# Two MLP layers behind windowed attention: the first four tiles' softmax divided after the product with the values

## The chip, the cores and the metric

The kernel runs on one core of one Trainium2 chip. The metric is the device time of one execution in microseconds (us), the median of several runs. The engines are TensorE (PE: matrix products; PEld is its loading of weights), VectorE (DVE), ScalarE (ACT), GpSimd (POOL) and SyncE (SP, which issues the DMA transfers). Each works through its own list of instructions in order and waits on semaphores for the others.

## The reference

```python
def _attn_ref(q, k, v):              # 4 batches, 8 heads, 576 positions, 64 per head
    ...
    mask = (rel >= 0) & (rel < 64)   # a window of 64 positions
    scores = np.where(mask, scale * (q @ k^T), -1e9)
    attn = np.exp(scores - max(scores))
    attn = attn / (sum(attn) + 1e-09)
    return attn @ v

def reference(...):
    x = attention output as (2304 tokens, 512)
    x = (s * relu(x @ moe_w_in)**2 + b) @ moe_w_out       # 512 -> 2048 -> 512
    h = x @ moe2_w_in
    return np.maximum(0.01 * h, h) @ moe2_w_out           # 512 -> 2048 -> 512
```

The weights arrive as 64-bit floats and are turned into 32-bit ones on the chip. Products are made as three passes of rounded parts (high by high, high by low, low by high), so that the result keeps 32-bit accuracy.

## The kernel before

**Tiles.** Attention is computed in 18 tiles of 128 tokens. Tile i goes through these operations, whose names the planner uses: `lq`, `lk`, `lv` (loads), `sc` (scores on PE, in two groups g of four heads), `mm` (DVE: mask and minimum, one instruction per head), `exp` (ACT, one per head, with the row's sum taken along by `accum_out`), `inv` (DVE: add 1e-9, reciprocal), `norm` (multiply by the reciprocal), `tp` (PE: transpose the weights of attention), `tt` (ACT: copy them to SBUF as `pt`), `pv` (PE: the product with the values, which leaves x transposed in PSUM as `xps`), `xh` (ACT: rounded high part of x) and `xl` (DVE: the rest). For the first four tiles (`early`, the first block of 512 tokens) `norm` is one DVE instruction per group (`normalise_four`); for later tiles it is eight ACT instructions.

**Steps of the first layer.** The first layer works in steps: one block of tokens by one chunk of 128 hidden units, 16 chunks. Step s makes `h` (lines 525 to 535: eight products with the high weights, four with the low), `e` 0 to 3 (ACT and DVE in turn: relu, square and scale, high part, low part) and `y` (lines 555 to 568: twelve products into four accumulators). Block 0 runs chunks 0 to 7, then block 1 all 16, then block 0 the rest. Each chunk's weights are loaded once (`lw`), converted (`cv` 0 on ACT, `cv` 1 to 4 on DVE, lines 451 to 470) and split into `wh` (ACT, line 487) and `wl` (DVE, line 493). Step s < 8 therefore needs chunk s freshly converted; the steps of block 1 that follow, 8 to 15, use the same eight chunks again.

**What sets the order.** `Order.emit` is a planner: every operation has an engine, an estimated duration, a rank (`key`, lower goes first), what it comes after, and the buffers that it takes. The planner plays the program through with these estimates and emits, on each engine, the ready operation of lowest rank. `self.fill(...)` tells the PE's gaps to `fill`, which puts products of zeros (line 1115) into a gap, until step 7's first activation is emitted. The PSUM pool "a" has four buffers: one is held by the `warm` tile of the zeros until step 0's second accumulator is done, two are used by `sc` of tiles 1 and 3, and `xps` of the first four tiles takes one each.

**Chunk 0** is loaded and converted in two halves, so its instructions are 512 wide and not 1024. `raw` has two buffers, so a chunk's load waits for the conversion of the chunk two before.

Of the kernel before, what the change touches and what calls it, by code (L numbers as in the profile page):

```python
# [15 lines left out]
P = 128  # L16
H, D = 8, 64
# [109 lines left out]
def kernel(  # L127
# [35 lines left out]
    sbt = const.tile([P, 2], F32, name="sbt")  # L163
    ydr = dramp.tile([P, KD, T], F32, name="ydr")
# [40 lines left out]
    EARLY = BLOCKS1[0] // P  # L205
    q_t, k_t, v_t, s_t, sc_t, sum_t, nmax_t, x_t, pt_t, tp_t = ({} for _ in range(10))
# [103 lines left out]

# [23 lines left out]
    def add_attention(i, b, t0, key):  # L334
# [17 lines left out]
        add(name("lv"), "sp", 1600, key - 4, lambda: load_v(i),  # L352
# [7 lines left out]
        for g in range(2):  # L360
            add(name("sc", g), "pe", 700, key - 6, lambda g=g: scores(i, g, sc),
# [5 lines left out]
            for j in range(4):  # L367
                add(name("mm", g, j), "dve", 172, key - 4.87, lambda g=g, j=j: mask_max(i, g, j),
                    [name("sc", g)] + ([name("mm", 0, 0)] if g + j else after_v) + [("masks",)],
                    first if g + j == 0 else (), [("sc", i, j % 2), ss, ("sm", i)])  # L370
                add(name("exp", g, j), "act", 480, key - 3.07, lambda g=g, j=j: exponent(i, g, j),
                    [name("mm", g, j)], use=[ss, ("sm", i)])

            if i < 2:
# [6 lines left out]
            if early:  # L381
# [8 lines left out]
            add(name("tp", g), "pe", 560, key - 2.96, lambda g=g: transpose_pe(i, g, tp),  # L390
                norm + [("masks",)], [(tp, "tp", i, g)], [ss])
            add(name("tt", g), "act", 478, key - 5.69, lambda g=g: take_transposed(i, g),
# [3 lines left out]
            add(name("pv", g), "pe", 620, key - 1, lambda g=g: values(i, g, xt),  # L396
                last + [name("lv")] + ([name("pv", 0)] if g else []),
                () if g else [(xt, "xt", i)], [("xt", i), ("v", i), pt])
        if i >= IN_W:
# [5 lines left out]
        add(name("xh"), "act", 478, key - 0.1, lambda: split_x_hi(i, b, t0),  # L405
# [3 lines left out]
        add(name("xl"), "dve", 602, key - 0.1, lambda: split_x_lo(i, b, t0),  # L409
# [193 lines left out]
    def add_step(s):  # L603
# [4 lines left out]
        for j in range(halves):  # L608
# [4 lines left out]
            add(("h", s, 0, j), "pe", 1820 * fj, s - 0.6, lambda c0=c0, c1=c1: emit_h(s, 0, c0, c1),  # L613
                [w_done["wh", l, c, 0]] + xs + ([("h", s, 1, j - 1)] if j else []),
                () if j else [("h", "h", s)], [("h", s), hi, *x])
            add(("h", s, 1, j), "pe", 910 * fj, s - 0.6, lambda c0=c0, c1=c1: emit_h(s, 1, c0, c1),
                [w_done["wl", l, c, 0], ("h", s, 0, j)], (), [("h", s), lo, *x])
        add(("e", s, 0), "act", 60 + 420 * f, s - 0.9, lambda: activate(s, 0),
            [("h", s, 1, halves - 1)], [("g", k, s) for k in ("r", "gh", "gl")], [("h", s)])
        add(("e", s, 1), "dve", 60 + 600 * f, s - 0.9, lambda: activate(s, 1),  # L620
            [("e", s, 0), ("sbt",)], use=[("r", s)])
        add(("e", s, 2), "act", 100 + 500 * f, s - 0.9, lambda: activate(s, 2),
            [("e", s, 1)], use=[("r", s), ("gh", s)])
        add(("e", s, 3), "dve", 60 + 600 * f, s - 0.9, lambda: activate(s, 3),
# [4 lines left out]
        if c0 < c < c1 - 1:  # L629
            both = [("y", s, 0), ("y", s, 1)]  # L630
            add(both[0], "pe", 2 * count * ns, s + 0.5,
# [469 lines left out]
    def masks():  # L1101
        make_masks()
        make_identity(nc, ident)

# [35 lines left out]
    for c in range(KF):  # L1140
        key = first_step[0, c, "w"] - 2.5
        if c == 0:
            add_weights(0, c, 0, 1, key - 4, -10.21)
            add_weights(0, c, 1, 2, key - 3.75, -11.71)
        else:
            add_weights(0, c, 0, 2, key + (-0.16 if c < 4 else 0))
# [3 lines left out]
    for b, n in enumerate(BLOCKS1):  # L1150
        for j in range(n // P):
            if b == 0:
                key = 1.0 * j - 6
            elif b == 1:
                key = 2 * j + 1.75
            else:
                key = first_step[0, 2] - 10 + 2 * (i - IN_W)
# [84 lines left out]
```

## Time and profile before

| | |
|---|---|
| median of 3 runs | 840.34 us (839.98 to 841.68) |
| the profiled execution's own time | 838.37 us |
| its span | 836.6 us |
| busy share of the span | PE 99%, PEld 88%, DVE 72%, ACT 53%, POOL 0% |
| first product of the first layer starts | 32.17 us |
| DMA | 194.65 MB, mean 233 GB/s |

The span runs from the first instruction to the last; what lies around it is 1.77 us. Busy shares are means over stages with different limits: DVE's 72% holds stretches where it has no gap. In a row of the time line, the first number is the start, the second the duration until the last result is out, and in brackets stands the idle time before it and what ended that. Two instructions that follow each other on one engine overlap at their ends, so the cost of one is read from start to start. In a view by windows the columns are: stretch in us, its length, then busy us (and instructions) of PE, PEld, DVE, ACT and POOL, the granted clock of TensorE as a share of its higher level of 2.4 GHz, the DMA share and GB/s. In a view by groups they are: line, engine, operation, names and shapes, count | busy us, mean ns of one | idle us before it and what ended it. A 32-bit product with small operands shows as two records, each with its own load of weights.

### The profile page before, as it was taken

To read this page: it belongs to the slowest core of one execution; us is meant where nothing else is said; L and a number is where in the kernel's file an instruction comes from. 1 tells how busy PE (TensorE), PEld (TensorE's weight loads), DVE (VectorE), ACT (ScalarE), POOL (GpSimd) and SP (SyncE) were. 2 spreads that over 40 slices of the span, in tenths; PEclk is the share of its full clock that TensorE was granted. 3 is DMA by queue.
4 is the path that set the end of the run, shared out by engine and by line. 5 is a ranking of instruction groups with operands and counts; after the bars stand their busy time and mean duration, and the time that the engine had idled before them with its cause. 6 is when DMAs were issued, how large, how long until landed. Compare 5 with 4: busy or idle time off the path is not lost.

```text
span 836.6 us, 14149 instructions
## 1 busy us (share of the span) xinstructions
PE 826.1 (99%) x5289; PEld 735.7 (88%) x5289; DVE 600.5 (72%) x1095; ACT 445.7 (53%) x960; POOL 3.5 (0%) x13
## 2 busy tenths in 40 slices
PE   7999999999999999999999999999999999999998
PEld 4677888877777788888889999999999999999998
DVE  5999998556565756776878876699456688365963
ACT  5999655466776776443446433356332355222443
POOL 1000000000000000000000000000000000000000
PEclk9999999999999999999999999999999999999999
DMA  9763544438478564757388489899977898988783
GB/s 314 290 234 112 191 156 154 138 114 284 140 233 265 160 205 152 260 180 238 108 290 274 152 282 386 277 314 288 318 255 249 269 312 285 293 253 251 251 265 114
DMA packets 85909, 194.65 MB, mean 233 GB/s; under 512 B 7121, under 2 KB 50129, under 8 KB 81873
## 3 DMA queue, kind: packets, MB, share of 16 engines
q1 hardware_dynamic: 85840, 193.75, 69.7%
q8 instruction: 42, 0.69, 0.3%
q14 instruction: 27, 0.21, 0.1%
HBM read 151.26 MB, written 42.47 MB: 232 GB/s over the span
## 4 chain that ended last, share of the span: by engine, by line
PE 92%; DMA 2%; ACT 2%; DVE 2%; issue 1%; SPq 0%; ACTq 0%
PE acc L567 24%; PE hps L532 23%; PE xps L900 22%; PE zps L900 12%; PE yps L900 5%; PE xps L305 2%; PE sc L249 2%; PE tp L288 2%; DMA w2dr<-raw 1%; DMA x2l<-ydr 1%; DMA kt<-in_k 1%; PE warm L1115 1%; ACT pt L294 0%; DVE x2s L827 0%; ACT s L267 0%
## 5 line engine op out<-in xcount | busy, mean ns | idle before, releaser
L567 PE MATMUL acc<-gh,wh 128*128 128x512 f32 (+1 forms) x320 | 118.1, 375 | 0.0
L532 PE MATMUL hps<-xh,wh 128*128 128x512 f32 (+1 forms) x324 | 117.6, 370 | 0.1
L532 PE MATMUL hps<-xl,wh 128*128 128x512 f32 (+1 forms) x324 | 116.4, 367 | 0.0
L567 PE MATMUL acc<-gh,wl 128*128 128x512 f32 (+1 forms) x320 | 116.2, 369 | 0.0
L900 PE MATMUL xps<-x2h,ws 128*128 128x384 f32 x384 | 106.1, 334 | 0.4 <-ACT part L923 0.4
L796 ACT ACTIVATE g2s<-g 128x768 fp32r<-128x768 f32 x84 | 70.9, 847 | 64.0 <-PE xps L900 40.4
L923 ACT ACTIVATE part<-xps 128x384 f32<-128x384 f32 x90 | 44.1, 490 | 110.1 <-PE xps L900 110.0
L799 DVE TENSOR_TENSOR g2s<-g,g2s 128x768 fp32r<-128x768 f32 x84 | 80.1, 954 | 31.5 <-ACT g2s L796 30.7
L900 PE MATMUL xps<-g2s,ws 128*128 128x384 f32 x576 | 102.3, 334 | 0.1
L900 PEld LDWEIGHTS xps<-g2s,ws 128*128 128x128 f32 x576 | 99.9, 188 | 0.7 <-ACT part L923 0.7
L546 DVE SCALAR_TENSOR_TENSOR r<-r,sbt 128x512 f32<-128x512 f32 (+1 forms) x80 | 55.3, 691 | 44.0 <-ACT r L544 43.5
L567 PE MATMUL acc<-gl,wh 128*128 128x512 f32 (+1 forms) x320 | 86.1, 373 | 0.0
L544 ACT ACTIVATE r<-hps 128x512 f32<-128x512 f32 (+1 forms) x80 | 44.1, 551 | 78.6 <-PE hps L532 78.4
L532 PE MATMUL hps<-xh,wl 128*128 128x512 f32 (+1 forms) x324 | 80.6, 370 | 0.0
L551 DVE SCALAR_TENSOR_TENSOR gl<-r,sbt,gh 128x512 fp32r<-128x512 f32 (+1 forms) x80 | 55.5, 694 | 26.7 <-ACT gh L549 26.5
L532 PEld LDWEIGHTS hps<-xh,wh 128*128 128x128 f32 x324 | 61.1, 189 | 11.5 <-ACT wh L487 0.9
L900 PEld LDWEIGHTS xps<-x2h,ws 128*128 128x128 f32 x384 | 70.1, 188 | 0.7 <-ACT part L923 0.7
L567 PEld LDWEIGHTS acc<-gh,wh 128*128 128x128 f32 x320 | 60.3, 189 | 11.6 <-DVE st L594 0.7
L532 PEld LDWEIGHTS hps<-xl,wh 128*128 128x128 f32 x324 | 61.1, 189 | 9.8
L567 PEld LDWEIGHTS acc<-gh,wl 128*128 128x128 f32 x320 | 60.4, 189 | 9.4
L549 ACT ACTIVATE gh<-r,sbt 128x512 fp32r<-128x512 f32 (+1 forms) x80 | 54.0, 674 | 26.0 <-DVE r L546 26.0
L567 PEld LDWEIGHTS acc<-gl,wh 128*128 128x128 f32 x320 | 56.5, 189 | 10.7 <-issue 0.9
(93 smaller groups left out, 1395.9 us busy)
## 6 DMA issues: line engine op xcount, KB each, us to landing
ws<-w1dr SPq DMA_DIRECT2D x84, 512.0 KB, 4.6
ws<-w2dr SPq DMA_DIRECT2D x84, 512.0 KB, 4.6
raw<-in_w SPq DMA_DIRECT2D x31, 1024.0 KB, 5.1
w1dr<-raw SPq DMA_DIRECT2D x16, 512.0 KB, 5.0
w2dr<-raw SPq DMA_DIRECT2D x16, 512.0 KB, 4.1
kt<-in_k SPq DMA_DIRECT2D x14, 384.0 KB, 5.0
vs<-in_v SPq DMA_DIRECT2D x10, 512.0 KB, 3.8
out<-st SPq DMA_DIRECT2D x24, 192.0 KB, 4.2
```

What stands on the lines that cost most here:

```text
L249: nc.tensor.matmul(out=sc_t[i][r][D * a:D * a + D, p, :], lhsT=q_t[i][D * r:D * r + D, p, D * a:D * a + D], rhs=k_t[i][D * r:D * r + D, p, ...
L288: nc.tensor.transpose(tp_t[i, g][:, j, :], s_t[i][:, g, j, :], ident)
L532: nc.tensor.matmul(out=hps_t[s][:, c0:c1], lhsT=w[:, 0, kk * P:kk * P + P], rhs=x[l, b][:, kk, c0:c1], start=(kk == 0 and j == 0 and part ...
L544: nc.scalar.activation(out=r, in_=hps_t[s], func=ACTF.Relu)
L546: nc.vector.scalar_tensor_tensor(out=r, in0=r, scalar=sbt[:, 0:1], in1=r, op0=ALU.mult, op1=ALU.mult)
L549: nc.scalar.activation(out=gh, in_=r, func=ACTF.Identity, bias=sbt[:, 1:2])
L551: nc.vector.scalar_tensor_tensor(out=gl, in0=r, scalar=sbt[:, 1:2], in1=gh.bitcast(F32), op0=ALU.add, op1=ALU.subtract)
L567: nc.tensor.matmul(out=acc_t[r, m], lhsT=three[j][0], rhs=three[j][1], start=(c == c0 and j == 0), stop=(c == c1 - 1 and j == 2))
L796: nc.scalar.activation(out=out, in_=in_, func=ACTF.Copy)
L799: nc.vector.tensor_tensor(out=out, in0=in_, in1=hi.bitcast(F32), op=ALU.subtract)
L900: nc.tensor.matmul(out=out, lhsT=w_[:, wcut], rhs=x_, start=(opens and j == k == 0), stop=(j == n - 1 and k == 2), skip_group_check=not opens)
L923: nc.scalar.activation(out=t, in_=bank_t[(*key, "x")], func=ACTF.Copy)
```

## The change

For the first four tiles (`BY_Q = EARLY`) the attention weights are no longer divided before they are transposed. `values_q` multiplies the undivided weights with the values the other way round, so that the queries stand on the partitions of `xq`, and multiplies them with a column of ones as well, which gives the row sums in `qsum`. `normalise_x` (DVE) adds 1e-9, takes the reciprocal and multiplies `xq` by it, into SBUF; `transpose_x` (PE) turns the result into `xps`. `exponent` no longer takes the sum along for these tiles. The planner's ranks, and its estimate for these `exp`, are other numbers throughout. Later tiles are computed as before.

```diff
@@ exponent
-        bias=nmax_t[i][:, g, j:j + 1], accum_out=sum_t[i][:, g, j:j + 1])
+        bias=nmax_t[i][:, g, j:j + 1],
+        **({} if i < BY_Q else {"accum_out": sum_t[i][:, g, j:j + 1]}))
...
+    def values_q(i, g):
+        if g == 0:
+            xq_t[i] = ps["a"].tile([P, H, D], F32, tag="a", name="xq")
+            qsum_t[i] = ps["a"].tile([P, H], F32, tag="a", name="qsum")
+        for h in range(4 * g, 4 * g + 4):
+            for out, rhs in ((xq_t[i][:, h, :], None), (qsum_t[i][:, h:h + 1], ones)):
+                for a in range(2):
+                    nc.tensor.matmul(
+                        out=out[D * a:D * a + D], lhsT=pt_t[i][:, a, h, :],
+                        rhs=v_t[i][:, a, h * D:h * D + D] if rhs is None else rhs,
+                        start=True, stop=True)
+
+    def normalise_x(i, part):
+        t = sum_t[i].rearrange("q g j -> q (g j)")
+        if part == 0:
+            nc.vector.tensor_scalar(out=t, in0=qsum_t[i], scalar1=1.0e-9, scalar2=None, op0=ALU.add)
+            nc.vector.reciprocal(out=t, in_=t)
+        else:
+            nc.vector.tensor_tensor(
+                out=s_t[i][:, 0].rearrange("q j k -> q (j k)").rearrange("q (h d) -> q h d", h=H),
+                in0=xq_t[i], in1=t.unsqueeze(2).to_broadcast([P, H, D]), op=ALU.mult)
+
+    def transpose_x(i):
+        x_t[i] = ps["a"].tile([P, KD, P], F32, tag="a", name="xps")
+        for kk in range(KD):
+            nc.tensor.transpose(x_t[i][:, kk, :], s_t[i][:, 0, kk, :], ident)
...
@@ add_attention
+        if i < BY_Q:
+            add(name("qinv"), "dve", 360, key - 0.8, lambda: normalise_x(i, 0),
+                [name("vq", 0), name("vq", 1)], use=[("qsum", i), ("sm", i)])
+            add(name("qnorm"), "dve", 640, key - 0.8, lambda: normalise_x(i, 1),
+                [name("qinv")], use=[("xq", i), ("sm", i), ss])
+            add(name("pv", 0), "pe", 560, key - 0.7, lambda: transpose_x(i),
+                [name("qnorm")], [("a", "xt", i)], [ss, ("xt", i)])
...
@@ ranks: of the first block's tiles, and of the step's first operation on ACT
-                key = 1.0 * j - 6
+                key = 1.35 * j - 6
...
-        add(("e", s, 0), "act", 60 + 420 * f, s - 0.9, lambda: activate(s, 0),
+        add(("e", s, 0), "act", 60 + 420 * f, s - 2.53, lambda: activate(s, 0),
```

On PE, before, tiles 2 and 3 go through transposes (`tp`) and the product with the values (`xps<-pt,vt`) like this, with tile 4's scores behind them:

```order
L1115 MATMUL warm<-zeros 128x512
L305 MATMUL xps<-pt,vt 64x64 x16
L288 MATMUL tp<-ident,s 128x128 x8
L1115 LDWEIGHTS zeros
L1115 MATMUL warm<-zeros 128x512
L305 MATMUL xps<-pt,vt 64x64 x16
L249 MATMUL sc<-kt,qt 64x128 x16
```

Now the same place reads, from the last products of tile 2 to the first products of the first layer (`xq` and `qsum` are the values and the row sums, the pair repeats eight times per tile, `xps<-ident,s` is the transpose of the divided x):

```order
L324 MATMUL qsum<-ones,pt 64x1 x2
L293 MATMUL tp<-ident,s 128x128 x4
L342 MATMUL xps<-ident,s 128x128 x4
L324 MATMUL xq<-vt,pt 64x64 x2
L324 MATMUL qsum<-ones,pt 64x1 x2
L324 MATMUL xq<-vt,pt 64x64 x2
```

A tile has 16 products with the values as before, 16 with the ones besides, and four transposes, and no zeros stand between them.

On DVE, before, between the masks of tile 3 and the low part of tile 0's x (`xl_410`), tile 2's softmax (`sum_284`, `s_283`) and chunk 0's conversion (`tmp_167`, `wl_419`) stand:

```order
L273 TENSOR_SCALAR sum_284<-sum_284 128x8
L274 RECIPROCAL sum_284<-sum_284 128x8
L281 TENSOR_TENSOR s_283<-s_283,sum_284 128x512 x2
L493 TENSOR_TENSOR wl_419<-tmp_167,wh_393 128x512
L456 TENSOR_SCALAR tmp_167<-tmp_167 128x512
L460 TENSOR_SCALAR tmp_167<-tmp_167 128x512
L464 SCALAR_TENSOR_TENSOR tmp_167<-raw_136,tmp_167 128x512
L468 SCALAR_TENSOR_TENSOR tmp_167<-raw_136,tmp_167 128x512
L323 TENSOR_TENSOR xl_410<-xps_274,xh_409 128x4x128
```

Now the row sums and products of tiles 1, 2 and 3 (`qsum_408`, `xq_465` and so on; `xl_430` is the low part of x) follow there one behind the other:

```order
L356 TENSOR_TENSOR xl_430<-xps_399,xh_429 128x4x128
L332 TENSOR_SCALAR sum_179<-qsum_408 128x8
L333 RECIPROCAL sum_179<-sum_179 128x8
L544 TENSOR_TENSOR wl_318<-tmp_170,wh_306 128x512
L335 TENSOR_TENSOR s_178<-xq_407,sum_179 128x512
L332 TENSOR_SCALAR sum_259<-qsum_466 128x8
L333 RECIPROCAL sum_259<-sum_259 128x8
L335 TENSOR_TENSOR s_258<-xq_465,sum_259 128x512
L356 TENSOR_TENSOR xl_430<-xps_510,xh_429 128x4x128
L332 TENSOR_SCALAR sum_371<-qsum_520 128x8
L333 RECIPROCAL sum_371<-sum_371 128x8
L335 TENSOR_TENSOR s_370<-xq_519,sum_371 128x512
```

DVE's multiplication reads PE's product, where before PE's transposes read DVE's multiplication.

## Rows read from the trace of the kernel before

**Rows 1.** Windows by stage, from the start to 300 us:

```profile
0.00:9.64 9.64, 5.46 (x47) 2.35 (x51) 2.37 (x18) 2.41 (x5) 3.49 (x13) 1.00 0.72 223
9.64:22.00 12.36, 11.90 (x158) 7.04 (x157) 10.24 (x58) 10.54 (x49) 0.00 (x0) 0.86 1.05 393
22.00:32.17 10.17, 8.39 (x126) 5.57 (x124) 9.93 (x37) 9.63 (x31) 0.00 (x0) 1.00 0.79 297
32.17:82.49 50.32, 50.20 (x425) 39.26 (x425) 49.77 (x112) 46.70 (x125) 0.00 (x0) 1.00 0.54 192
82.49:300.00 217.51, 217.51 (x1456) 174.48 (x1455) 149.91 (x339) 142.30 (x362) 0.00 (x0) 1.00 0.57 186
```

**Rows 2.** Groups of PE up to the first accumulation at 44.83 us, by form:

```profile
L1115 PE MATMUL warm<-zeros 128*128 128x512 bf16 x45 | 14.4, 459 | 1.0 <-DVE zeros L1135 1.0
```

**Rows 3.** Time line of PE at the start of step 7:

```profile
81.45 1.07 PE L567 MATMUL acc<-gl,wh 128*128 128x512 f32 x4
82.49 0.50 PE L532 MATMUL hps<-xh,wh 128*128 128x512 f32 x1
```

**Rows 4.** Time line of ACT, high part of chunk 7:

```profile
81.38 1.06 ACT L487 ACTIVATE wh<-tmp 128x1024 fp32r<-128x1024 f32 x1 [0.54 <-DVE tmp L468]
```

**Rows 5.** Time line of DVE, prologue, and the last conversion of chunk 7:

```profile
10.24 0.29 DVE L261 CUSTOM_DVE_ANT_0 s<-sc,mask 128x128 f32<-128x128 f32 x1 [0.61 <-PE sc L249]
...
12.03 0.17 DVE L273 TENSOR_SCALAR sum<-sum 128x4 f32<-128x4 f32 x1
...
13.05 0.42 DVE L460 TENSOR_SCALAR tmp<-tmp 128x512 uint32<-128x512 uint32 x1
...
21.77 0.29 DVE L261 CUSTOM_DVE_ANT_0 s<-sc,mask 128x128 f32<-128x128 f32 x1 [0.76 <-PE sc L249]
...
21.98 0.28 DVE L261 CUSTOM_DVE_ANT_0 s<-sc,mask 128x128 f32<-128x128 f32 x1
...
22.62 0.17 DVE L273 TENSOR_SCALAR sum<-sum 128x8 f32<-128x8 f32 x1
...
23.05 1.29 DVE L281 TENSOR_TENSOR s<-s,sum 128x512 f32<-128x512 f32 x2
...
24.27 0.68 DVE L493 TENSOR_TENSOR wl<-tmp,wh 128x512 fp32r<-128x512 f32 x1
...
24.87 0.42 DVE L456 TENSOR_SCALAR tmp<-tmp 128x512 f32<-128x512 f32 x1
...
27.12 0.68 DVE L323 TENSOR_TENSOR xl<-xps,xh 128x512 fp32r<-128x512 f32 x1
...
80.12 1.22 DVE L468 SCALAR_TENSOR_TENSOR tmp<-raw,tmp 128x1024 uint32<-128x1024 uint32 x1
```

**Rows 6.** Time line of PE, scores, transposes and values of the first tiles:

```profile
18.08 0.67 PE L249 MATMUL sc<-kt,qt 64*64 64x128 f32 x16
...
18.68 0.66 PE L288 MATMUL tp<-ident,s 128*128 128x128 f32 x4
...
19.27 0.67 PE L249 MATMUL sc<-kt,qt 64*64 64x128 f32 x16
...
33.31 1.15 PE L305 MATMUL xps<-pt,vt 128*64 128x64 f32 x32
...
34.39 1.10 PE L249 MATMUL sc<-kt,qt 64*64 64x128 f32 x32
```

**Rows 7.** Time line of ACT, exponents with their sums, and plain multiplications:

```profile
9.07 0.39 ACT L267 ACTIVATE s<-s,nmax 128x128 f32<-128x128 f32 x1
...
9.46 0.38 ACT L267 ACTIVATE s<-s,nmax 128x128 f32<-128x128 f32 x1
...
38.25 2.44 ACT L278 ACTIVATE s<-s,sum 128x128 f32<-128x128 f32 x8
```

**Rows 8.** Windows around the stretch in which the granted clock is lower:

```profile
10.90:14.00 3.10, 3.10 (x14) 1.04 (x8) 2.95 (x19) 2.50 (x14) 0.00 (x0) 0.50 1.04 395
14.00:18.00 4.00, 3.70 (x60) 2.65 (x58) 3.67 (x14) 2.82 (x12) 0.00 (x0) 0.98 1.07 388
```

More of the change, by code (lines that the diff above doesn't have):

```diff
@@ L163 @@
     sbt = const.tile([P, 2], F32, name="sbt")
+    ones = const.tile([P, 1], F32, name="ones")
     ydr = dramp.tile([P, KD, T], F32, name="ydr")
@@ L205 @@
     EARLY = BLOCKS1[0] // P
+    BY_Q = EARLY
+    xq_t, qsum_t = {}, {}
     q_t, k_t, v_t, s_t, sc_t, sum_t, nmax_t, x_t, pt_t, tp_t = ({} for _ in range(10))
@@ L351, in add_attention @@
                 [name("lk", 0)] if n else [], () if n else rk, [("k", i)], delay=1900)
-        add(name("lv"), "sp", 1600, key - 4, lambda: load_v(i),
+        add(name("lv"), "sp", 1600, key - 2.27, lambda: load_v(i),
             [("lw", 0, KF - 1, 0, 2)] if i == IN_W else
@@ L360, in add_attention @@
         for g in range(2):
-            add(name("sc", g), "pe", 700, key - 6, lambda g=g: scores(i, g, sc),
+            add(name("sc", g), "pe", 700, key - 6.53, lambda g=g: scores(i, g, sc),
                 [name(x, g if early else 0) for x in ("lq", "lk")]
@@ L367, in add_attention @@
             for j in range(4):
-                add(name("mm", g, j), "dve", 172, key - 4.87, lambda g=g, j=j: mask_max(i, g, j),
+                add(name("mm", g, j), "dve", 172, key - 5.16, lambda g=g, j=j: mask_max(i, g, j),
                     [name("sc", g)] + ([name("mm", 0, 0)] if g + j else after_v) + [("masks",)],
                     first if g + j == 0 else (), [("sc", i, j % 2), ss, ("sm", i)])
-                add(name("exp", g, j), "act", 480, key - 3.07, lambda g=g, j=j: exponent(i, g, j),
+                add(name("exp", g, j), "act", 300 if i < BY_Q else 480, key - 2.44, lambda g=g, j=j: exponent(i, g, j),
                     [name("mm", g, j)], use=[ss, ("sm", i)])
-            if i < 2:
+            if i < BY_Q:
+                pass
+            elif i < 2:
                 add(name("inv", g), "dve", 360, key - 3, lambda g=g: invert(i, g, g + 1),
@@ L380, in add_attention @@
             inv = name("inv", g if i < 2 else 0)
-            if early:
+            if i < BY_Q:
+                norm = [name("exp", g, j) for j in range(4)]
+            elif early:
                 norm = [name("norm", g)]
@@ L395, in add_attention @@
             last = [name("tt", g)]
-            add(name("pv", g), "pe", 620, key - 1, lambda g=g: values(i, g, xt),
+            if i < BY_Q:
+                add(name("vq", g), "pe", 800, key - 1, lambda g=g: values_q(i, g),
+                    last + [name("lv"), ("masks",)] + ([name("vq", 0)] if g else []),
+                    () if g else [("a", "xq", i), ("a", "qsum", i)],
+                    [("xq", i), ("qsum", i), ("v", i), pt])
+                continue
+            add(name("pv", g), "pe", 620, key - 1.09, lambda g=g: values(i, g, xt),
                 last + [name("lv")] + ([name("pv", 0)] if g else []),
                 () if g else [(xt, "xt", i)], [("xt", i), ("v", i), pt])
+        if i < BY_Q:
+            add(name("qinv"), "dve", 360, key - 0.8, lambda: normalise_x(i, 0),
[4 more added lines that the diff above has]
+                [name("qnorm")], [("a", "xt", i)], [ss, ("xt", i)])
+            add(name("pv", 1), "none", 0, key, lambda: None, [name("pv", 0)])
         if i >= IN_W:
@@ L404, in add_attention @@
             return
-        add(name("xh"), "act", 478, key - 0.1, lambda: split_x_hi(i, b, t0),
+        add(name("xh"), "act", 478, key + 0.02, lambda: split_x_hi(i, b, t0),
             [name("pv", 0), name("pv", 1)] + ([("xh", i - t0 // P)] if t0 else []),
@@ L408, in add_attention @@
             [("xt", i), ("xh", 0, b), ("xl", 0, b)])
-        add(name("xl"), "dve", 602, key - 0.1, lambda: split_x_lo(i, b, t0),
+        add(name("xl"), "dve", 602, key - 0.92, lambda: split_x_lo(i, b, t0),
             [name("xh")], use=[("xt", i), ("xh", 0, b), ("xl", 0, b)])
@@ L630, in add_step @@
             both = [("y", s, 0), ("y", s, 1)]
-            add(both[0], "pe", 2 * count * ns, s + 0.5,
+            add(both[0], "pe", 2 * count * ns, s + 0.35,
                 lambda: [emit_y(s, m, (0, 1)) for m in range(count)],
@@ L1103, in masks @@
         make_identity(nc, ident)
+        nc.gpsimd.memset(ones, 1.0)
     WARM = 10
```

26 lines of the change are left out of this document (13 added, 13 removed).

## The prediction

> **What bounds the kernel now.** The windows by stage come first. PE's busy time equals the length of the stretch from 82.49 to 300 us, and of the 50.32 us ahead of that only 0.12 are missing [rows 1]; work that PE has behind 82.49 us can only be moved as a whole, by beginning it sooner. What is not needed lies in the prologue: idle time in the first three stretches, and products of zeros, 45 up to 44.83 us [rows 2]. So the question is what sets the moment at which step 7, the last that needs a freshly converted chunk, can start. The time line of PE shows it start at 82.49 us, when the products before it, started at 81.45, are just through [rows 3]; the time line of ACT shows the high part of chunk 7 run from 81.38 us for 1.06 us, to 82.44, after ACT had waited 0.54 us for DVE [rows 4]; and DVE's conversion that it waited for began at 80.12 us and took 1.22 [rows 5]. PE and DVE arrive together, and DVE cannot give way: from 22 us to 82.49 its stretches lack 0.24 and 0.55 us of busy time [rows 1]. Before, from 9.64 us to 22, it lacks 2.12 us. DVE's list up to that conversion is therefore a sum that ends last: its work, plus 2.12 + 0.24 + 0.55 = 2.91 us of idle time.
>
> **The change on DVE: work removed.** The list up to the last conversion of chunk 7 holds the same masks, conversions, steps and low parts in both orders; only the first four tiles' division differs. Tiles 0 and 1 did it per group, from 12.03 to 13.05 us, 1.02 each, so 2.04 a tile; tiles 2 and 3 from 22.62 to 24.27 us, 1.65 a tile [rows 5]. Together 2 x 2.04 + 2 x 1.65 = 7.38 us. Now a tile has one sum with reciprocal, 22.62 to 23.05 = 0.43 us, and one multiplication of 512 elements, half of 23.05 to 24.27 = 0.61 us [rows 5], taken the same from PSUM: 4 x 1.04 = 4.16 us. Removed: 3.22 us.
>
> **The change on PE: work added, on the way to DVE.** A group of eight products with the values costs half of 33.31 to 34.39 us, 0.54 us, 34 ns a record [rows 6]. The eight products with the ones have one moving column instead of 64. No row shows one. The nearest rows say that the columns do not count here: scores with 128 columns go at 18.68 - 18.08 = 0.60 us for 16 records, 37 ns each [rows 6]. I take the ones at 34 ns a record too, 0.54 us a group, so that a group costs 1.08 and a tile 2.16 us. From below the bound is zero (0.54 a group); from above I take twice, for the lower clock [rows 8]. Four transposes cost 0.59 us (18.68 to 19.27) [rows 6].
>
> The Trainium skill ("TensorE: Matmul & The Clock Gate", Part 1, "Wait — 56ns, not 53.3ns?") says that start-to-start never falls below about 25 ns however few columns there are. By that floor a group of ones would cost 0.40 us as an estimate, and the sum below would come out 1.1 us lower, at 839.6 us; the row's 34 ns is for products with 64 columns, so no run here shows which holds.
>
> **The walk.** What counts is where DVE stands idle for PE. ACT begins exponents at 9.07 us. With the sum one takes 0.39 us; without it I take the plain multiplication's 2.44 / 8 = 0.305 [rows 7]. Eight of them and one eviction (0.5) bring ACT to 12.0 us, three more to 12.9, when tile 0's second group can be transposed. PE is then at half its clock, 0.50 from 10.9 to 14 us [rows 8]: that transpose ends at 14.15, tile 1's at 14.75, tile 2's second scores at 15.35. DVE, done with the conversion since 14.5, has waited 0.9 us. It does four masks at 0.21 (21.77 to 21.98) and a low part at 0.60 (24.27 to 24.87) [rows 5], to 16.85. PE does the first group of tile 0's values, a transpose and the second group: 15.35 + 1.08 + 0.59 + 1.08 = 18.1 us. DVE's wait: 1.3 us. Then 1.04 for the division, 0.45 of conversion, eight masks 1.7, to 21.3 us. PE's next values, of tile 1, need the PSUM buffers that tile 3's scores hold until these masks are through (four buffers, one held by the zeros): 21.45 to 23.6 us. Meanwhile DVE has conversions of 1.8 (the four parts take 24.87 to 27.12 = 2.25 [rows 5], and 0.45 was done) and tile 0's low part, to 23.74; no wait. Tile 2's values wait for the buffer of tile 1's row sums, 24.25 to 26.4 us; DVE, with a low part of the weights and one multiplication, is done at 25.4 and waits 1.07. Tile 3's values need tile 2's buffers: 27.6 to 29.76 us. DVE waits 0.7 for ACT's high part of tile 1 and 1.05 for tile 3's row sums. Behind that it has work in hand again: tile 4's scores are through before it asks for them.
>
> The new waits sum to 0.9 + 1.3 + 1.07 + 0.7 + 1.05 = 5.02 us. Of the 2.12 us before 22 us, those ahead of 11.2 stay, 0.7 with the wait of 0.61 at 10.24; the wait of 0.76 at 21.77 and the rest go [rows 5]. The 0.79 behind 22 us stay. New idle time: 5.02 + 0.7 + 0.79 = 6.5 us against 2.91, so +3.6 us. With the 3.22 removed, DVE's list ends **0.4 us later**. PE itself is not late: its first products of the first layer follow tile 3's values and a transpose at about 30.4 us, against 32.17 now (where the third stretch ends [rows 1]), and the 11 zeros that the order has ahead of step 1 cost it about 0.5 us in front of chunk 1's weights, which it regains behind them.
>
> **What costs nothing.** ACT is spared 32 sums of 0.08 us, 2.6 us; it is ahead of PE in the walk (tile 3's last exponent ends near 25.3 us, its transpose comes at 26.4), so this buys nothing by itself. On SP's queue tile 0's values move ahead of the second half of chunk 0's weights, which comes behind 1.5 MB more, at 393 GB/s [rows 1] 3.8 us later; ACT asks for it only near 17.6 us, and all transfers up to chunk 1 are the same bytes. POOL's column of ones is set behind the masks, ten microseconds ahead of its first use. The later ranks, with tiles 8 to 17 nearer to each other, fall into a stretch in which PE is busy throughout and ACT for 142.30 of 217.51 us, 65% [rows 1]; if ACT were late with one high part there, PE would wait for a fraction of its 0.6 us.
>
> **The sum.** 838.37 us (the profiled execution: span 836.6 and 1.77 around it) + 0.4 = 838.8 us. The median of the runs shown is 1.97 us above that execution, so the forecast for a median is 840.34 + 0.4 = **840.7 us**.
>
> **Rivals.**
> 1. *The ones are cheap, and PE is early enough to feed DVE: faster.* If the ones cost nothing, each of the four values shrinks by 1.08 us, and the waits of 1.3, 1.07 and 1.05 us shrink or go. The bound is that all new idle time goes and the 3.22 us stay: 837.1 us; with half of it, 838.7. For it: PE and DVE are level at 82.49 us, so that both must be earlier, and PE is, by 1.8 us at its first product. Against it: 34 and 37 ns a record at 64 and 128 columns.
> 2. *PE stays at the lower clock: slower.* Place: PE, 14 to 18 us. The granted clock is at 0.50 from 10.9 to 14 us [rows 8], behind a first stretch in which PE was busy for 5.46 of 9.64 us [rows 1], and is back behind it, with PE busy for all of the 3.10 us, mostly on zeros. The order now has a single product of zeros there, between short real products. If the clock is still 1.2 GHz in tile 0's values, their 2.16 us and a transpose take 2.75 us more, DVE's wait grows by as much, and nothing behind returns it: 840.7 + 2.7 = 843.4 us. It decides over the forecast as soon as the stretch from 14 to 18 us is at half clock for more than about 1.3 us. Against it: if the real products take twice the time at half the clock, they fill the stretch as the zeros did.
> 3. *The change is not on the way at all:* PE's line decides and not DVE's. PE then is earlier by a few tenths behind step 1: about 840.0 us, no change either.
>
> **How the numbers follow.** No change, within 0.2% (1.7 us, about what a measurement of this kernel can tell): the forecast, 0.50, and the third rival, 0.05, together 0.55, from 838.7 to 842.0 us. Faster (the first rival): 0.27, since the price of the ones has no row of its own and the walk's waits add up its errors. Slower (the second, or ones dearer than the values): 0.18. The range takes in most of the first rival and half of the second: 838.2 to 842.8 us; the forecast's own range is 839.6 (the floor of 25 ns) to 842.0.
>
> **What would show it.** Right: step 7's first product within a microsecond of 82.5 us; DVE idle for 5 us or more between 14 and 31 us, released by PE's row sums and by ACT's high part; a group of values with ones at about 1.08 us; the granted clock back at 1.00 by about 14.5 us. Wrong: a record of the ones far under 34 ns; DVE without a gap from 20 us on; the clock at 0.50 beyond 15 us; or PE waiting in steps 1 to 7 for something other than converted weights, such as tile 4's or 5's x.

## The result, and the profile after

The changed kernel takes **852.57 us** (median of 4 runs, 850.53 to 855.62) beside 840.16 us of the kernel before in the same comparison: ratio 1.0149, 95% interval 1.0118 to 1.0179. It is slower by 12.4 us, where 840.7 us and a range of 838.2 to 842.8 were forecast. The profiled execution took 855.62 us (span 853.8), the longest of the four, so what is read from it is somewhat larger than in the median. One execution of e11 below, of 2096.49 us, belongs to a slower state of the chip and is left out of its row.

The windows of the changed kernel by the same stages, cut where its step 0 and its step 7 begin (columns as in [rows 1]); the last row takes the stretch up to step 7 as a whole:

```profile
9.64:22.00 12.36, 11.29 (x190) 8.90 (x182) 9.13 (x57) 10.89 (x32) 0.00 (x0) 0.89 1.03 377
22.00:33.70 11.70, 10.09 (x208) 9.54 (x206) 6.01 (x15) 5.61 (x13) 0.00 (x0) 0.81 0.89 347
33.70:90.44 56.74, 53.17 (x435) 41.18 (x433) 52.41 (x126) 46.86 (x127) 0.00 (x0) 0.98 0.44 155
90.44:300.00 209.56, 207.66 (x1383) 166.67 (x1384) 145.44 (x318) 134.45 (x335) 0.00 (x0) 1.00 0.55 178
...
9.64:90.44 80.80, 74.55 (x827) 59.62 (x819) 67.56 (x196) 63.36 (x171) 0.00 (x0) 0.94 0.59 217
```

DVE, the third busy column, lacks 80.80 - 67.56 = 13.24 us up to step 7, where it lacked 2.91 before. It has 69.94 - 67.56 = 2.38 us less work, the 69.94 being the three stretches of [rows 1]. Idle time of +10.33 and work of -2.38 make up the 7.95 us by which step 7 is late: 90.44 against 82.49 us [rows 3]. Behind step 7 PE now lacks 1.90 us by 300 us, where it lacked nothing.

The time line of PE at step 7, the answer to [rows 3]; the bracket is the idle time before the row and what ended it:

```profile
88.79 1.07 PE L618 MATMUL acc<-gl,wh 128*128 128x512 f32 x4
90.44 0.50 PE L583 MATMUL hps<-xh,wh 128*128 128x512 f32 x1 [0.58 <-ACT wh L538]
```

PE and DVE no longer arrive together: PE waits for converted weights. The largest of the waits that make up DVE's 13 us, on its time line in the prologue, as in [rows 5]:

```profile
17.57 0.17 DVE L332 TENSOR_SCALAR sum<-qsum 128x8 f32<-128x8 f32 x1 [1.11 <-PE qsum L324]
...
20.15 0.29 DVE L265 CUSTOM_DVE_ANT_0 s<-sc,mask 128x128 f32<-128x128 f32 x1 [1.11 <-PE sc L253]
...
28.45 0.17 DVE L332 TENSOR_SCALAR sum<-qsum 128x8 f32<-128x8 f32 x1 [2.67 <-PE qsum L324]
...
33.05 0.17 DVE L332 TENSOR_SCALAR sum<-qsum 128x8 f32<-128x8 f32 x1 [2.20 <-PE qsum L324]
...
37.15 0.29 DVE L265 CUSTOM_DVE_ANT_0 s<-sc,mask 128x128 f32<-128x128 f32 x1 [1.74 <-PE sc L253]
```

Every one of these waits is for PE. PE's own time line in that stretch:

```profile
19.74 0.43 PE L253 MATMUL sc<-kt,qt 64*64 64x128 f32 x4 [0.86 <-issue]
...
24.76 0.31 PE L324 MATMUL xq<-vt,pt 128*64 128x64 f32 x4
...
24.99 0.31 PE L324 MATMUL xq<-vt,pt 128*64 128x64 f32 x4
...
27.62 0.27 PE L324 MATMUL xq<-vt,pt 128*64 128x64 f32 x1 [1.61 <-issue]
...
30.30 0.46 PE L324 MATMUL xq<-vt,pt 128*64 128x64 f32 x4
...
30.73 0.46 PE L324 MATMUL xq<-vt,pt 128*64 128x64 f32 x4
```

Two things are seen. A head (four records of values, four of ones) takes 24.99 - 24.76 = 0.23 us, 29 ns a record on average over both. And PE stands twice, for 0.86 and 1.61 us, for nothing that the profile shows ("issue"). Behind the second stop a head takes 0.43 us (30.30 to 30.73), and the windows show the clock there:

```profile
26.00:28.00 2.00, 0.39 (x15) 0.39 (x14) 0.00 (x0) 0.00 (x0) 0.00 (x0) 1.00 1.00 412
28.00:30.00 2.00, 2.00 (x34) 1.82 (x31) 1.06 (x3) 0.96 (x2) 0.00 (x0) 0.83 0.98 392
30.00:32.00 2.00, 2.00 (x42) 2.00 (x42) 0.69 (x1) 1.15 (x2) 0.00 (x0) 0.50 1.05 417
...
34.00:36.00 2.00, 2.00 (x17) 1.77 (x19) 1.41 (x3) 0.60 (x1) 0.00 (x0) 0.50 0.00 0
```

The granted clock (third number from the right) is 0.50, the lower of the two levels, from some 29 to 36 us, after a stretch in which PE was busy for 0.39 of 2 us. In the kernel before it was at 1.00 from 22 us on [rows 1].

Step 7 is 8 us late in this execution, the second layer begins 16 us late. The rest lies in the first layer's later steps. PE's largest waits from 85 to 480 us (total, number, longest); the profiled execution of the kernel before has none:

```profile
PE acc L618 <- DVE st L645: 3.1, 2, 2.1
PE acc L618 <- ACT gh L600: 1.6, 1, 1.6
PE sc L253 <- ACT xo L468: 0.9, 2, 0.6
```

One of them in full, by the time line of all engines:

```profile
362.60 0.35 SPq L722 DMA_DIRECT2D raw<-in_w  x1
...
363.04 1.09 SPq L652 DMA_DIRECT2D ydr<-st  x2
...
369.15 1.12 ACT L505 ACTIVATE flt<-raw 128x1024 f32<-128x1024 f32 x1 [5.23 <-DMA raw<-in_w]
369.82 0.69 DVE L645 COPY st<-acc 128x512 f32<-128x512 f32 x1 [4.44 <-DMA ydr<-st]
370.18 0.58 ACT L595 ACTIVATE r<-hps 128x512 f32<-128x512 f32 x1
...
370.56 0.75 PE L618 MATMUL acc<-gh,wh 128*128 128x512 f32 x1 [2.07 <-DVE st L645]
```

SP issues a load of second-layer weights at 362.60 us and two stores of results right behind it. ACT's list has the conversion of that load (L505) ahead of the step's own activation (L595), and stands for 5.23 us; DVE's list has a copy that needs the buffer of a store, and stands for 4.44 us; PE stands behind DVE. Behind this wait the granted clock is lower once more, 0.50 from 370.7 to 374.0 us.

### The profile page after: what moved, and what is told of

Read it like the earlier page. It is cut to its first block, busy times and chain, and to the rows that moved or that the text cites. A ratio compares the mean times of both kernels' runs of the same rounds, so it can differ in the third digit from the quotient of the medians.

```text
span 853.8 us, 14361 instructions
## 1 busy us (share of the span) xinstructions
PE 833.6 (98%) x5413; PEld 745.7 (87%) x5413; DVE 599.2 (70%) x1087; ACT 442.6 (52%) x928; POOL 3.5 (0%) x14
## 4 chain that ended last, share of the span: by engine, by line
PE 80%; DMA 10%; ACT 4%; DVE 3%; issue 2%; SPq 0%; ACTq 0%; DVEq 0%
PE xps L951 23%; PE hps L583 18%; PE acc L618 17%; PE zps L951 11%; PE yps L951 6%; DMA raw<-in_w 4%; DMA w1dr<-raw 3%; PE sc L253 1%; DMA ydr<-st 1%; PE tp L293 1%; PE xps L310 1%; DMA w2dr<-raw 1%; PE xq L324 1%; ACT vs L271 1%; DMA kt<-in_k 1%
## 5 line engine op out<-in xcount | busy, mean ns | idle before, releaser
L595 ACT ACTIVATE r<-hps 128x512 f32<-128x512 f32 (+1 forms) x80 | 44.0, 550 | 75.3 <-PE hps L583 75.1
```

Source lines behind the costliest of these rows:

```text
L595: nc.scalar.activation(out=r, in_=hps_t[s], func=ACTF.Relu)
```

## The experiments

Ratios are to the kernel before, run beside each on the same chip (medians of 838.4 to 840.7 us), with 95% intervals. Step 7 is its first product in the profiled execution (82.49 us before, 90.44 after).

| run | what it is | median us | ratio | step 7 |
|---|---|---|---|---|
| e1 | change, later ranks old | 847.79 | 1.0087 (1.0054 to 1.0121) | 87.19 |
| e2 | before, later ranks new | 844.63 | 1.0066 (1.0041 to 1.0091) | 81.66 |
| e3 | change, all ranks old | 851.38 | 1.0140 (1.0110 to 1.0170) | 87.00 |
| e4 | changed, without the ones | 846.04 | 1.0077 (1.0053 to 1.0101) | 84.10 |
| e5 | before, new ranks of later steps | 842.53 | 1.0020 (0.9999 to 1.0041) | 82.37 |
| e6 | before, new ranks of tiles 8 to 17 | 839.01 | 0.9989 (0.9969 to 1.0008) | 81.97 |
| e7 | e1 and six products of zeros | 845.53 | 1.0068 (1.0041 to 1.0095) | 87.04 |
| e8 | e1 planned anew without ones | 841.46 | 1.0015 (0.9994 to 1.0035) | 84.39 |
| e9 | e2, transfers planned longer | 864.49 | 1.0283 (1.0250 to 1.0315) | 82.28 |
| e10 | e1, ones twice | 851.70 | 1.0133 (1.0088 to 1.0178) | 97.19 |
| e11 | before, low parts on POOL | 852.29 | 1.0157 (1.0117 to 1.0196) | 88.73 |
| e12 | e2, loads alone planned longer | 861.55 | 1.0280 (1.0248 to 1.0311) | 82.66 |

**Two losses or one? (e1, e2)** The theory was two separate losses, one in the prologue and one from the later ranks; the rival, that the later waits only pass on the first.

```diff
 # e1: the changed kernel, for the later steps and tiles (e2: its complement, on the kernel before)
-        add(("e", s, 0), "act", 60 + 420 * f, s - 2.53, ...
+        add(("e", s, 0), "act", 60 + 420 * f, (s - 2.53 if s < 8 else s - 0.9), ...
-                key = first_step[0, 2] - 10.39 + 1.38 * (i - IN_W)
+                key = first_step[0, 2] - 10 + 2 * (i - IN_W)
```

> The changed kernel with the old ranks for steps 8 and later and for tiles 8 to 17; the prologue (tiles 0 to 7, steps 0 to 7, weights) keeps the change and the new ranks. Theory, two separate causes: the prologue costs 8 us (step 7 at 90.4 us against 82.5) and the later ranks of the first layer the rest. Then PE has no waits behind 82 us as in the kernel before, the delay of 8 us is carried to the end unchanged, and the time is 848 us. Rival, one cause: the later waits are transfers pushed late by the prologue; then they come back, and the time stays at 852.6 us.

> The kernel before, with its own softmax and prologue ranks, but the new ranks for steps 8 and later and for tiles 8 to 17. Theory, two separate causes: step 7 starts at 82.5 us as before, and delays open behind it in the stretches 206 to 216, 330 to 342 and 360 to 380 us, where PE's accumulations wait for DVE's stagings and ACT's gh: 840.2 + (12.4 - 8) = 844.6 us, up to 848. Rival, one cause in the prologue: 840.2 us, no new wait.

Both times came as the theory said: 847.79 and 844.63 us. (In e1's profiled execution, of 845.54 us, step 7 is 4.70 us late and not 8.) The two excesses, 0.87% and 0.66%, add up to 1.53%, and the change has 1.49%. The windows of e1 behind 22 us:

```profile
22.00:31.96 9.96, 8.47 (x209) 7.88 (x209) 6.04 (x18) 5.97 (x13) 0.00 (x0) 1.00 1.00 385
...
9.64:87.19 77.55, 72.61 (x830) 57.40 (x826) 67.50 (x196) 63.92 (x172) 0.00 (x0) 0.98 0.63 228
```

This is the same order of the prologue as the changed kernel's, but with the clock at 1.00 from 22 us to step 0. DVE's idle time is 10.05 us, not 13.24, and step 7 starts 3.25 us earlier: that is about what the lower clock cost in the other execution. The place of the lower clock is known for the profiled executions alone, but the mean granted clock of every execution is on record: 0.992 in all four of the changed kernel, 0.992 to 0.997 in e1's seven, of which the profiled one has the highest, and 0.995 to 1.000 in the kernel before's 21 beside e1. In e2 PE waits, from 85 us on, where it did in the changed kernel:

```profile
PE acc L618 <- ACT gh L600: 1.5, 1, 1.5
PE acc L618 <- DVE st L645: 1.0, 2, 0.5
```

Ahead of the first of these ACT stands for a load, on the time line:

```profile
312.54 1.12 ACT L505 ACTIVATE flt<-raw 128x1024 f32<-128x1024 f32 x1 [4.05 <-DMA raw<-in_w]
...
317.88 0.50 PE L618 MATMUL acc<-gh,wh 128*128 128x512 f32 x1 [1.55 <-ACT gh L600]
```

Between the two, ACT's list has the step's first activation, a tile's eight exponents (314.05 to 317.13 us) and only then the `gh` that PE waits for.

**The change alone (e3)** keeps the division and the products with ones, and sets all ranks back.

```diff
-                key = 1.35 * j - 6
+                key = 1.0 * j - 6
 ...
-            add(name("sc", g), "pe", 700, key - 6.53, ...
+            add(name("sc", g), "pe", 700, key - 6, ...
```

> The changed division of the first four tiles, with all ranks as before. Theory: the ones products themselves cost the prologue its time (PE waits for nothing that the trace shows, for 0.86, 1.61 and 0.78 us, and then runs at half clock), so step 7 starts at 87 to 90 us and the time is 845 to 848 us, with no later waits. Rival: the prologue's new ranks are at fault (they took the products of zeros out of PE's stream): step 7 at 82 to 83.5 us, 840 to 841 us.

Step 7 starts at 87.00 us, as the theory said, so the new ranks of the prologue aren't at fault. But the time is 851.38 us, beyond both, with a mean clock of 0.998 in all six executions: the planner writes the whole order from its own clock, and a prologue that ends elsewhere gives another order later, which waits too. From 85 to 480 us PE waits 2.1 us for ACT's transposed tiles and 2.5 us for DVE:

```profile
PE xps L310 <- ACT pt L299: 2.1, 5, 0.9
PE acc L618 <- DVE st L645: 1.5, 1, 1.5
PE acc L618 <- DVE gl L602: 1.0, 1, 1.0
```

**Without the ones (e4)**: the order of the changed kernel, row for row, less its products with ones. The exponents on ACT give the sums again.

```diff
-        for out, rhs in ((xq_t[i][:, h, :], None), (qsum_t[i][:, h:h + 1], ones)):
+        for out, rhs in ((xq_t[i][:, h, :], None),):
```

> The changed kernel in its own order, without the 128 products with the ones: the sums come from the exponents on ACT, as before. Theory: the stalls are PE running out of instructions, because the ones double the instructions in that stretch; then the waits of 0.86, 1.61 and 0.78 us shrink below 0.3 us together, step 0 starts 3.6 us of products and 2.5 us of waits earlier at about 28 us, step 7 at about 84 us, and the time is 852.6 - 6 = 846.5 us (the later ranks still cost theirs). Rival: the waits stand at fixed places of the program whatever is issued around them: they stay, the granted clock falls behind them as well, and step 7 starts at 87 us or later, 849 us or more.

846.04 us, step 0 at 29.2, step 7 at 84.10: the ratio falls from 1.0149 to 1.0077, so some 6 us of the 12.4 go with the ones. The waits of 0.86 and 1.61 us are gone; a third, of 0.78 us at 38.82 ahead of tile 5's scores, stays (0.77), so it has another cause. A tile's values now take 1.08 us, from 27.71 to 28.79; with the ones, at the same clock, they take 2.12 in e1 (29.43 to 31.55):

```profile
27.71 1.15 PE L324 MATMUL xq<-vt,pt 128*64 128x64 f32 x32
28.79 0.66 PE L342 MATMUL xps<-ident,s 128*128 128x128 f32 x4
...
9.64:84.10 74.46, 70.42 (x702) 52.98 (x702) 67.62 (x197) 66.49 (x203) 0.00 (x0) 0.98 0.65 237
```

DVE still lacks 74.46 - 67.62 = 6.84 us up to step 7 (last row).

**What stops PE? (e7, e10)** The theory was that PE runs out of instructions, which come in blocks.

```diff
 # e7
         for h in range(4 * g, 4 * g + 4):
+            if (i, h) == (2, 5):
+                product_of_zeros(idle["warm"], 6)
 # e10
-            for out, rhs in ((xq_t[i][:, h, :], None), (qsum_t[i][:, h:h + 1], ones)):
+            for out, rhs in ((xq_t[i][:, h, :], None), *[(qsum_t[i][:, h:h + 1], ones)] * 2):
```

> The kernel with the change and the new prologue ranks, later ranks old (847.8 us), plus six products of zeros, 1.3 us of PE, put right ahead of the product of tile 2's values at which PE stood 1.34 us for nothing that the trace shows. Theory: PE ran out of instructions there, so the zeros, 12 instructions in 1.3 us, give the supply time: the wait shrinks to below 0.3 us, step 0 and step 7 start as without them (32.0 and 87.2 us), and the time stays at 847.8 us. Rival: the wait is tied to the place or to another event: it stays at 1.2 us or more, step 7 comes 1 to 1.3 us later, 849 us.

> The changed kernel with old later ranks (847.8 us), each of the 128 products with the ones issued twice: 256 more products on PE, 512 records with their weight loads. Theory: PE gets its instructions in blocks of 256 records, and under the weight loads' traffic a block takes 6.5 to 8 us whatever is in it (waits stood ahead of records 449, 705 and 961); two more blocks delay step 0 by 12 to 14 us, from 32.0 to about 45 us, with waits for nothing shown at records 449, 705, 961 and 1217, and the time is 858 to 862 us. Rival: the products cost their 29 ns each and nothing more: 7.4 us, step 0 at 39.4 us, 855 us.

In e7 the wait did not shrink. It moved into the zeros, three of which ran before it:

```profile
25.39 0.82 PE L1169 MATMUL warm<-zeros 128*128 128x512 bf16 x3
27.78 0.82 PE L1169 MATMUL warm<-zeros 128*128 128x512 bf16 x3 [1.57 <-issue]
```

So it doesn't belong to the instruction ahead of which it was first seen. (Step 7 is at 87.04 us, as the theory had it and not 1 us later, and with 845.53 us the six zeros cost nothing that can be told.) It belongs to a count: the windows up to the first stop and from there to the second hold the same numbers of products and weight loads (first and second bracket) in three kernels. The changed kernel:

```profile
0.00:19.00 19.00, 15.66 (x217) 10.09 (x218) 9.56 (x58) 11.74 (x31) 3.52 (x14) 0.91 0.89 294
19.00:27.00 8.00, 6.08 (x127) 5.35 (x126) 5.57 (x25) 5.46 (x15) 0.00 (x0) 1.00 1.01 395
```

The same windows of e1:

```profile
0.00:19.60 19.60, 16.14 (x217) 10.47 (x218) 9.59 (x58) 12.00 (x32) 3.52 (x14) 0.91 0.87 293
19.60:27.30 7.70, 6.08 (x127) 5.35 (x126) 5.54 (x24) 5.18 (x14) 0.00 (x0) 1.00 1.02 392
```

And of e7:

```profile
0.00:18.90 18.90, 14.75 (x217) 9.14 (x218) 9.58 (x58) 11.92 (x32) 3.52 (x14) 1.00 0.88 288
18.90:27.20 8.30, 6.67 (x127) 5.45 (x126) 5.53 (x24) 5.11 (x14) 0.00 (x0) 1.00 1.03 408
```

217 + 218, then 127 + 126, whatever the instructions are; with the sequencer's own instructions (waits and branches), 449 and then 256 more. That speaks for a supply in blocks. The traces add that a kernel which gets to these counts later does not stop there. The three go on behind the counts at 19.35 to 20.07 us and at 27.62 to 27.78 us. The kernel before gets there at 23.26 and 33.60 us and e4 at 22.65 and 30.84, both without a stop; so does e3, with all its ones, at 19.43 and 27.72. e10 passes the first at 20.06 us and stops at the second alone, for 0.27 us, up to 26.25. By this reading the ones stop PE because they bring it to the counts early. Open is a wait of e3, 0.68 us for nothing shown at 26.16 us, behind neither count. The wait of 0.78 us isn't of this kind: in e7 it stands ahead of the same scores (0.76 us), six products further on.

That a block always takes 6.5 to 8 us, so that two more cost 12 to 14 us, as the expectation of e10 had it, fell: e10 took 851.70 us and not 858 to 862. That expectation also counted wrongly. The program has 64 products with ones, which the trace shows as 128 records; doubled, they are 128 records more, not 256. At 29 ns that makes 3.7 us, and the medians differ by 851.70 - 847.79 = 3.9. The plain price is enough to explain it, but the test is weak: by the two intervals the difference is uncertain by some 4.7 us (an estimate), and the mean granted clock of e10's executions goes from 0.984 to 0.996, so one more block of 6.5 us isn't ruled out by the medians. (The profiled execution of e10 is its longest, 858.37 us, with a granted clock of 0.51 from 26 to 42 us, which makes up most of the 10 us by which its step 7, at 97.19, is later than e1's.)

**Is the division itself dear? (e8)** e1's ranks, without the ones and without their PSUM buffer, planned anew.

```diff
-            qsum_t[i] = ps["a"].tile([P, H], F32, tag="a", name="qsum")
 ...
-            nc.vector.tensor_scalar(out=t, in0=qsum_t[i], scalar1=1.0e-9, ...
+            nc.vector.tensor_scalar(out=t, in0=t, scalar1=1.0e-9, ...
```

> The changed division with the sums on ACT, no products with ones and no PSUM buffer for them, planned anew so, with the new ranks in the prologue and the old ones later. Theory: without the ones the prologue loses no more than 1 us (DVE has 3.2 us less work, PE no stall), and later nothing: step 7 at 81.5 to 83.5 us, 838 to 841 us. Rival: the division behind the values costs in itself, since DVE waits for PE's values where it waited for nothing before: step 7 at 84 us or later (84.1 without the ones in the changed order), 841 to 844 us.

841.46 us: no change that can be told. Step 7 is at 84.39 us, the rival's number, though step 0 starts at 26.0 us, six earlier than before. DVE lacks 7.32 us up to step 7 (the third busy column against the length), so the 2.5 us of work that it is spared don't make up for its waits:

```profile
9.64:84.39 74.75, 72.29 (x718) 54.04 (x718) 67.43 (x196) 66.86 (x205) 0.00 (x0) 0.98 0.64 236
```

**Which of the later ranks? (e5, e6)** e2's edit, in two halves.

```diff
 # e5 has the steps' ranks (this line and its like) alone, e6 the tiles' alone
-        add(("e", s, 3), "dve", 60 + 600 * f, s - 0.9, ...
+        add(("e", s, 3), "dve", 60 + 600 * f, (s - 0.9 if s < 8 else s - 6.57), ...
```

> The kernel before with only the new ranks of steps 8 and later (h, e, y); attention as before. Theory: the step ranks are harmless (they only put a step's own work ahead of others), the loss of 5.7 us seen with all later ranks comes from the tiles: 838.9 to 840 us, no wait of PE over 0.5 us near 318 and 359 us. Rival: the step ranks cause it: 843 to 845 us, with PE waiting 1.5 us for ACT's gh near 318 us.

> The kernel before with only the new ranks of tiles 8 to 17 (1.38 steps apart, and the ranks inside a tile); steps as before. Theory: the tiles cause the loss: 843 to 845 us, with ACT's wait of 4 us for a load of second-layer weights (against 0.9 before) and PE waiting behind it. Rival: the step ranks cause it: 838.9 to 840 us. If both come out under 841 us, only the two together do it.

The theory that the tiles do it fell: alone they cost nothing (0.9989). The steps' ranks alone may cost a little (1.0020, interval to 0.9999). Only both together cost 0.66%. The waits of one execution do not tell the median: in e6's profiled one PE waits 3.6 us from 85 to 480 us, in e2's 3.0.

**Is it the wait in the list, or the transfer? (e9, e12)** The planner is told that transfers take longer, so that it writes what needs them further back. This also changes what some later loads find in DRAM, so part of the output is another; only the waits, and the end of the first layer, are read from these two.

```diff
-        add(name("lw2"), "sp", 3200, key, lambda: load_w2(u), after, [("big", *raw)], delay=1900)
+        add(name("lw2"), "sp", 3200, key, lambda: load_w2(u), after, [("big", *raw)], delay=4400)
 # e9 alone
-                [("leave", run, m)], use=[st], delay=1900)
+                [("leave", run, m)], use=[st], delay=4400)
```

> The kernel before with all new later ranks (844.6 us, 1.0066 of before), but the planner that writes the order is told that the loads of second-layer weights and the stores of the first layer take 2.5 us longer than it assumed. Theory: the loss comes from ACT's and DVE's queues holding an instruction that waits for a transfer (a load that ACT waited 4.0 us for near 312 us, stores that DVE waited 2.0 us for near 195 and 358 us) ahead of a step's own work; planned later, the waits of PE near 195, 318 and 359 us shrink below 0.5 us each and the time is 839 to 842 us. Rival: the transfers themselves come late, whatever stands ahead: 844 us or more.

> The kernel before with all new later ranks (844.6 us), the planner told 2.5 us more for the loads of second-layer weights alone; the stores as it assumed. Theory: the load that ACT waits for near 312 us, ahead of a step's own work, is the larger part: PE's wait of 1.55 us near 318 us goes, those of 0.5 us near 195 and 358 us for DVE's stagings stay, the first layer ends 1.5 to 3 us earlier than with the new ranks alone (484.4 us) and the time is 841 to 843 us. Rival: the stores are the larger part: the first layer ends at 484 us, 844 us or more.

In the first layer the theory held: in e9 PE waits 1.4 us in all from 85 to 480 us, and the last products of an h start at 478.84 us (478.76 before, 482.44 in e2); in e12 at 480.03, so by this measure the loads are the larger part, though PE has a new wait there, 1.8 us for ACT's `pt`. The times went the other way, 864.49 and 861.55 us, for a reason that neither side named: the weights prepared later reach the second layer late, where PE now waits for them, 14.2 us in all in e9, and before waited for none. So no run shows in its time that taking these waits away gives back what the ranks cost. PE's waits of e9 from 480 us on:

```profile
PE zps L951 <- DMA ws<-w1dr: 9.7, 3, 4.5
PE xps L951 <- DMA ws<-w1dr: 4.5, 3, 2.5
```

**A version faster than both? (e11)** DVE's list bounds the prologue and POOL is idle there, so seven of its subtractions were given to POOL.

```diff
+    POOLED = (1, 2, 3, 4, 5, 6, 7)
-        nc.vector.tensor_tensor(
+        (nc.gpsimd if c in POOLED else nc.vector).tensor_tensor(
             out=wl[l, c][:, j0:j1], in0=wf_t[l, c][:, j0:j1].bitcast(F32),
```

> The kernel before, with its own division and ranks; the low parts of the weight chunks 1 to 7, seven subtractions of 1.22 us on DVE, are done by POOL, which is idle behind 9.64 us. Theory: DVE's list is what ends last before step 7, so step 7 starts earlier by what DVE saves until ACT (6.0 us idle up to there) or PE takes over, 2 to 4 us: 835 to 838 us. Rival: POOL is too slow at it, or slows DVE through the memory that both read: PE waits for low parts in steps 1 to 7, 842 us or more.

The rival had the time, 852.29 us, and its second ground. POOL takes 2.5 us for what DVE did in 1.22, and meanwhile DVE's joining of the bits (L464) takes 1.64 us on average, where it took 1.23. The groups of e11 by form, from 44 to 89 us (mean ns before the last bar):

```profile
L493 POOL TENSOR_TENSOR wl<-tmp,wh 128x1024 fp32r<-128x1024 f32 x6 | 15.0, 2505 | 36.1 <-ACT wh L487 36.1
...
L464 DVE SCALAR_TENSOR_TENSOR tmp<-raw,tmp 128x1024 uint32<-128x1024 uint32 x5 | 8.2, 1640 | 0.2
```

The Trainium skill ("SBUF — State Buffer", "Who interferes with whom") says that a DVE instruction with two inputs in SBUF contends with POOL's reads, and this trace agrees: of the five L464, which read both their inputs there, the one beside POOL's subtraction at 53.66 us took 3.30 us, the other four 1.23. On DVE's time line each of the seven subtractions has beside it one instruction that takes 1.87 to 3.30 us, among them L456 and L460, which have one input (1.98 to 2.89 us, against 0.68 and 0.69 before). So DVE is busy for 73.42 us up to step 7, where it was for 69.94, though six subtractions are taken from it. PE's waits are for DVE then (2.4 us for a low part of x at 60.01) and hardly for POOL (0.2 us). No version that was run beats the kernel before; e6 comes nearest, and can't be told from it.

## Why the prediction was wrong

**What held.** It is the conversions of weights that set step 7, and not PE's own work: PE waits there for a high part (0.58 us). The price of the ones was about right: a group of values with ones was taken at 1.08 us and took 1.03 at full clock (14.81 to 15.84 us), with 29 ns a record where 34 were taken. That the columns do not count held as well: in e4, without ones, records of 64 columns also follow each other after 29 ns within a group. The floor of about 25 ns that the Trainium skill gives ("TensorE: Matmul & The Clock Gate", Part 1, "Wait — 56ns, not 53.3ns?") is not reached here. Up to 25 us the walk fits: tile 0's row sums at 17.57 us (18.1 forecast), tile 2's values at 24.51 (24.25). The work removed from DVE was forecast at 3.22 us and measured at 2.38.

**First failing step: the walk's waits.** New idle time of 6.5 us was forecast, 3.6 more than before, against 3.22 us of work less. It is 13.24 us in the profiled execution and 10.05 in e1, where the clock held; in e1 that is 7.14 more against 69.94 - 67.50 = 2.44 of work less, so step 7 is 4.70 us late and not 0.4. By terms, forecast and then measured in the changed kernel: tile 2's scores 0.9 and 0.15, tile 0's row sums 1.3 and 1.11, tile 3's scores none and 1.11, tile 2's row sums 1.07 and 2.67, tile 1's high part 0.7 and 0.57, tile 3's row sums 1.05 and 2.20, tile 4's scores none and 1.74. The walk let PE stand only for buffers and inputs. It stood 0.86 and 1.61 us for nothing that the trace shows, among tile 3's scores and among tile 2's values, and then, in the one execution, ran at half clock through tile 3's values and step 0, worth about 3.25 us (in e1 the last two waits are 0.75 and 0.79). The sentence "Behind that it has work in hand again" was wrong as well: DVE waits 1.74 us for tile 4's scores at 37.15. Without the ones (e4) the idle time is 6.84 us, near the forecast that was made with them; that is chance, since more of e4's waits are for ACT than for PE. The division behind the values, by itself, is a draw: e8 can't be told from the kernel before (1.0015), and of e4's 0.77% the later ranks alone make 0.66 (e2). The ones turn it into a loss, some 6 us in the changed order (e4). Their plain time is 3.7 us (128 records of 29 ns), and PE's two stops, which go with them, are 2.5.

**Second failing step: "The later ranks".** The prediction put them at nothing, or at a fraction of 0.6 us. They cost 0.66% alone (e2, some 5.5 us), about as much as e1 differs from the changed kernel, 4.8. The ground given, PE busy throughout and ACT 65% busy, was the wrong one to look at. ACT, DVE and SP work their lists in order, and the new ranks put an instruction that waits for a transfer ahead of a step's own work. That the ranks cost it is shown; that these waits are the way is argued from the profiled executions: in e2 PE waits behind them (1.55 us at 317.88), and in e9, where they are gone, the first layer ends where it did before. Such waits were there before, on the time lines of ACT and DVE, with enough slack behind them that PE never waited:

```profile
326.92 1.12 ACT L454 ACTIVATE flt<-raw 128x1024 f32<-128x1024 f32 x1 [2.99 <-DMA raw<-in_w]
...
354.88 0.69 DVE L594 COPY st<-acc 128x512 f32<-128x512 f32 x1 [2.03 <-DMA ydr<-st]
```

A mean busy share says nothing of them; these rows, had they been read, would have shown that the step could cost something.

**The rivals.** The first (ones cheap, hence faster) had its condition met in small part, 29 ns for 34, and its result not. The second had the right side, and PE at 1.2 GHz between short products, but the wrong place: from 14 to 18 us the clock was at 1.00, and it fell from 29 to 36 us. It isn't the main part, since e1's profiled execution, at full clock behind 22 us, still takes 845.54 us against 838.37; but with a mean clock of 0.992 in all four executions of the changed kernel, some of it is in the median. The third, that the change isn't on the way, fell with e1.

## What to carry to other kernels

When a bound engine is spared work by moving it behind another engine's product, add up the waits that this makes, and count the helper's instructions as well as their time (e4). Ranks that reorder a list without adding work aren't free: look in the trace of before for waits on transfers that are hidden now, and ask what comes behind each of them in the new order. And after any edit in front, compare the later order too, since a planner that keeps its own clock rewrites all of it (e3).

## What the hardware showed

A record of a 32-bit product with its own weight load took 29 ns at full clock, with a single moving column and with 64 alike: mostly 0.117 us for four records of 64 columns (e4), 0.233 for these and four of one column (e1), 0.350 for these and eight of one column (e10). PE stopped twice behind the same counts of records in three kernels, 435 and then 253 more, for 0.86 to 0.95 and 1.34 to 1.61 us, while the DMA engines were fully busy (share 1.01 to 1.03); kernels that reach these counts later, as the kernel before, show no such stop. That the stops are the supply of instructions is argued from the counts and times and not shown by a record of it. The granted clock fell to 0.50 behind the second stop in the changed kernel, and not in e1 and e7, which have a stop of about the same length in the same place. It fell behind a stop of only 0.27 us in e10, with PE busy for 3.72 of the 4 us from 22 to 26 us, and stayed at 0.51 from 26 to 42 us with PE busy for 15.75 of 16. What makes it fall is not shown.
